# Filter transposes of an FFT-convolution kernel: quarter TensorE tiles in place of half tiles, with a new emission order

## The chip, the cores and the metric

The kernel runs on one core of a Trainium2 chip. The metric is the device time of one execution in microseconds (us). Every run of a changed kernel was made beside runs of the kernel before on the same chip. The kernel before took 230.56 to 233.16 us in its first three runs, a spread of about 1%, so a difference of 1% needs several runs; where a verdict below has an interval, it is a 95% one.

## The reference, cut to what matters

One sequence of 2048 positions and 640 channels goes through two branches, and a gate for each position mixes them.

```python
def _A_ref(q, k, v, shift_k, ssm_k, ssm_D):      # branch A
    k_shift = ...                                 # 4-tap causal convolution of k
    kv  = k_shift * v
    kf_f = rfft(pad(ssm_k))                       # filter: 640 channels x 2048 taps
    y   = irfft(rfft(pad(kv)) * kf_f)[:S]         # long convolution, length 4096
    return q * (y + kv * ssm_D)

def _B_ref(x, w1, w2, w3, w4):                    # branch B
    h  = gelu(layernorm(x) @ w1)
    x1 = x + concat(shifts of h) @ w2
    return x1 + gelu(layernorm(x1) @ w3) @ w4

g = sigmoid((x * gate_w).sum(-1))                 # x = q
return g * A + (1 - g) * B
```

The change concerns the filter `ssm_k`, which arrives with channels on the partitions and is needed with time on the partitions before its DFT.

## The kernel before

The program first registers its steps (a name, what it may run on, its dependences, its buffers) and then emits them in the order of one long string, `ORDER`. An entry such as `mx2.2/V` is "step mx2.2, on VectorE"; `P` is TensorE, `A` ScalarE, `G` GpSimd, `S` the engine that issues DMA; further numbers are buffers. Every engine runs its own entries strictly in that sequence.

The filter lies in a tile of 5 blocks of 128 channels (`a`). A position splits into block half `g`, an index of 64 and `t1`. A transpose loads its input as the stationary operand of TensorE:

```python
HN = RG.rearrange("p (k a g t) -> p k t g a", k=DT, g=2, t=T1)   # 64 columns, 32 elements (64 bytes) apart
for a in range(DT):                                              # 5 blocks
    def f_trh(e, a=a, pb=pb):
        for t1 in range(T1):                                     # 16
            for g in range(2):                                   # the two column halves of the array
                nc.tensor.transpose(out=ps16(pb)[64 * g:64 * g + 64, t1 // 8, (t1 % 8) * P:(t1 % 8 + 1) * P],
                                    in_=HN[:, a, t1, g, :], identity=IDN[:])
    tr = pl.add("trh%d" % a, {PE: 16 * 64 + (0 if a else 600)}, f_trh, [ldh[a], n_idn], [pb], mode="c")
    trhe.append(evac("trhe%d" % a, ...))                         # PSUM to SBUF, VectorE or ScalarE
```

The first DFT step uses the array in four quarters of 64 rows by 64 columns, and all five evacuations must be done before it:

```python
for g in range(2):
    for C in range(2):
        nc.tensor.matmul(ps(pb)[64 * C:64 * C + 64, g, i * n:(i + 1) * n],
                         lhsT=F1[64 * g:64 * g + 64, s, 64 * C:64 * C + 64],
                         rhs=src[64 * g:64 * g + 64, s, ds], ...)
```

## Time and profile before

| | before |
|---|---|
| time, median of 3 runs | 232.64 us (230.56 to 233.16) |
| span of the profiled execution | 230.4 us |
| TensorE busy in the span | 211.5 us |
| filter transposes | 160, in 80 pairs |
| first matmul of the first DFT step | 18.89 us |
| first key-value product of VectorE ends | 57.8 us |

The times and instructions of the profile come from one execution. "L687" is a line of the kernel. Three lines of the TensorE groups between 5 and 27 us, kernel before: line, operation, tiles, count, then busy us and the mean ns of one, then idle time ahead of the group and what ended it.

```profile
L687 PE MATMUL PS<-IDN,RG 128*64 128x128 bf16 x160 | 9.4, 289 | 2.0 <-DMA RG<-in_A_ssm_k_dram 2.0
L564 PE MATMUL PS<-XNT,R 128*128 128x512 bf16 x23 | 6.0, 380 | 0.1
L535 PE MATMUL PS<-IDN,XN 128*128 128x128 bf16 x40 | 2.9, 220 | 0.0
```

L687 is the filter transpose, L535 the transposes of the layer norm, L564 the matmuls with w1. The only idle time of these is for the filter to arrive. Two more lines of the page will be compared later: the clock granted to TensorE in 40 slices, in tenths, and the DMA queue that brings instructions (number, MB, share).

```profile
PEclk9999999999999999999999999999999999999998
...
q8 instruction: 14, 0.23, 0.4%
```

### The profile page before, as it was taken

Reading aid. Unit: us, or ns where it says so; the run is one execution under the profiler, and the core shown is the slowest. Engines: PE = TensorE matmul, PEld = TensorE weight load, DVE = VectorE, ACT = ScalarE, POOL = GpSimd, SP = SyncE. Lnnn points to the kernel's source line nnn. Section 1 sums busy time; section 2 is a strip of 40 time slices with the busy share of each in tenths; the row PEclk is TensorE's granted clock in tenths of the full one; section 3 lists DMA queues with packets and bytes.
Section 4 is the critical chain, followed back from the end, with each engine's and each line's share of the span. In section 5 each row is a group of like instructions: output and inputs, shape, how many; then the busy total and the mean of one; then the engine's idle time right before and its main releaser. Section 6 shows DMA issues by size and latency. Waiting matters only on the chain.

```text
span 230.4 us, 4825 instructions
## 1 busy us (share of the span) xinstructions
PE 211.5 (92%) x1831; PEld 119.1 (52%) x1849; DVE 187.4 (81%) x324; ACT 158.2 (69%) x238; POOL 50.6 (22%) x129
## 2 busy tenths in 40 slices
PE   6698999999989999999999998889799999999960
PEld 6694556455644476544545564233246554567640
DVE  6869988579999999999997986968849994065874
ACT  6669993859695990289979433889875886545431
POOL 2654388632640695000023000000000000000000
PEclk9999999999999999999999999999999999999998
DMA  5999989999999999999899999999979965699896
GB/s 204 396 392 172 300 160 258 233 216 308 383 188 281 299 152 292 270 209 300 256 303 379 314 318 345 257 270 351 351 281 311 370 208 179 207 405 349 275 369 242
DMA packets 51095, 65.39 MB, mean 284 GB/s; under 512 B 20608, under 2 KB 37761, under 8 KB 50688
## 3 DMA queue, kind: packets, MB, share of 16 engines
q1 hardware_dynamic: 51072, 65.09, 96.7%
q8 instruction: 14, 0.23, 0.4%
q14 instruction: 9, 0.07, 0.1%
HBM read 37.03 MB, written 18.35 MB: 240 GB/s over the span
## 4 chain that ended last, share of the span: by engine, by line
PE 50%; DMA 28%; DVE 15%; SPq 3%; issue 3%; ACT 1%; DVEq 0%
PE PS L751 14%; PE PS L764 13%; DMA CJ<-in_A_q_dram 6%; PE PS L847 6%; DMA XNT<-XN 6%; PE PS L564 6%; DMA GHD<-SX 5%; DMA RK<-in_A_k_dram 4%; PE PS L687 4%; DMA RK<-GHD 4%; DVE RK L819 3%; PE PS L712 3%; DMA RG<-in_A_ssm_k_dram 3%; PE PS L653 2%; DVE QX L660 2%
## 5 line engine op out<-in xcount | busy, mean ns | idle before, releaser
L751 PE MATMUL PS<-XNT,W 128*128 128x512 bf16 x228 | 54.8, 380 | 2.0 <-DVE RK L819 0.8
L764 PE MATMUL PS<-W,RG 128*128 128x320 bf16 x384 | 55.7, 299 | 0.5 <-DVE QX L770 0.5
L316 ACT CAST SX<-PS 128x1024 bf16<-128x1024 f32 (+1 forms) x51 | 45.6, 933 | 13.4 <-PE PS L847 11.0
L764 PEld LDWEIGHTS <-RG 128*128 128x128 bf16 x384 | 36.5, 98 | 19.9 <-issue 6.0
L751 PEld LDWEIGHTS <-W 128*128 128x128 bf16 x240 | 21.8, 97 | 31.1 <-issue 7.6
L755 ACT ACTIVATE RG<-PS 128x512 bf16<-128x512 f32 x48 | 27.9, 607 | 10.7 <-PE PS L751 10.3
L770 DVE SCALAR_TENSOR_TENSOR QX<-PS,ZG,QX 128x320 bf16<-128x320 f32 x32 | 17.1, 544 | 11.7 <-PE PS L764 11.7
L898 DVE TENSOR_TENSOR SX<-SX,R 128x2048 bf16<-128x2048 bf16 x20 | 23.8, 1219 | 3.1 <-DMA R<-R 2.8
L564 PE MATMUL PS<-XNT,R 128*128 128x512 bf16 x94 | 23.1, 379 | 0.4 <-issue 0.2
L653 PE MATMUL PS<-R 128*128 128x320 bf16 x160 | 23.4, 299 | 0.0
L320 DVE CAST SX<-PS 128x1024 bf16<-128x1024 f32 (+1 forms) x17 | 18.0, 1063 | 4.0 <-PE PS L712 3.2
L942 ACT ACTIVATE RK<-PS,ZG 128x640 bf16<-128x640 f32 x16 | 11.7, 793 | 13.1 <-PE PS L932 5.9
L823 DVE TENSOR_TENSOR RK<-RK 128x1280 bf16<-128x1280 bf16 x24 | 20.0, 833 | 0.5
L653 PEld LDWEIGHTS <-R 128*128 128x128 bf16 x160 | 15.2, 98 | 8.2 <-issue 2.0
L819 DVE TENSOR_TENSOR RK<-RK,CJ 128x1280 bf16<-128x1280 bf16 x24 | 19.1, 816 | 0.0
L316 ACT CAST KV<-PS 128x1024 bf16<-128x1024 f32 x16 | 16.0, 1019 | 2.2 <-PE PS L847 2.1
L493 ACT ACTIVATE RG<-QX 128x640 bf16<-128x640 bf16 x16 | 11.8, 739 | 8.1 <-DVE QX L660 4.0
L520 DVE TENSOR_SCALAR XN<-QX,MV,RS 128x640 bf16<-128x640 bf16 x32 | 14.9, 476 | 2.5 <-DMA XNT<-XN 2.4
L318 ACT ACTIVATE R<-PS 128x1024 bf16<-128x1024 f32 x12 | 11.8, 1026 | 6.2 <-PE PS L847 4.6
L847 PEld LDWEIGHTS <-M 64*64 64x64 bf16 x320 | 7.6, 105 | 16.2 <-issue 7.1
L847 PE MATMUL PS<-RK,M 64*64 64x512 bf16 x160 | 13.1, 386 | 2.6 <-DMA RK<-GHD 1.7
L564 PEld LDWEIGHTS <-R 128*128 128x128 bf16 x100 | 9.0, 97 | 10.6 <-issue 1.3
(107 smaller groups left out, 269.5 us busy)
## 6 DMA issues: line engine op xcount, KB each, us to landing
GHD<-SX SPq DMA_DIRECT2D x8, 640.0 KB, 6.0
GXD<-SX SPq DMA_DIRECT2D x8, 640.0 KB, 4.7
RK<-GHD SPq DMA_DIRECT2D x4, 1280.0 KB, 8.8
RK<-GXD SPq DMA_DIRECT2D x4, 1280.0 KB, 7.6
R<-R SPq DMA_DIRECT2D x8, 640.0 KB, 7.5
VD<-KV SPq DMA_DIRECT2D x4, 1280.0 KB, 5.7
RK<-VD SPq DMA_DIRECT2D x8, 640.0 KB, 6.5
W<-in_B_w_dram SPq DMA_DIRECT2D x2, 1920.0 KB, 12.4
```

What stands on the lines that cost most here:

```text
L316: nc.scalar.copy(out=o, in_=i)
L320: nc.vector.tensor_copy(out=o, in_=i)
L564: nc.tensor.matmul(ps(pb), lhsT=lhsT, rhs=XNT[:, xb.idx, k, :], start=(k == 0), stop=(k == DT - 1))
L653: nc.tensor.matmul(ps(pb)[:, j, 0:DH], lhsT=gst_ap(k, s), rhs=W2[:, k, j * DH:(j + 1) * DH], start=(k == 0), stop=(k == DT - 1))
L751: nc.tensor.matmul(ps(pb), lhsT=W3[:, k, f0 * P:(f0 + 1) * P], rhs=XNT[:, xb.idx, k, :], start=(k == 0), stop=(k == DT - 1))
L755: gns.append(pl.add("g2.%d.%d" % (c, f0), {A: act_p(512)}, lambda e, f0=f0, pb=pb, gb=gb: nc.scalar.activation(out=GTP[:, gb.idx, f0 % 4, ...
L764: nc.tensor.matmul(ps(pb)[:, 0:DH], lhsT=GTP[:, gbs[f // 4].idx, f % 4, i * P:(i + 1) * P], rhs=W4[:, f, j * DH:(j + 1) * DH], start=(f == ...
L770: nc.vector.scalar_tensor_tensor(out=x, in0=ps(pb)[:, 0:DH], scalar=OMG[:, s:s + 1], in1=x, op0=ALU.mult, op1=ALU.add)
L819: m = pl.add("km%d.%d.%d" % (c, u, j), {V: dve(2 * D, .52)}, lambda e, src=src, cj=cj, tb=tb: nc.vector.tensor_tensor(out=TMP[:, tb.idx].r ...
L823: prev = pl.add("ka%d.%d.%d" % (c, u, j), {V: dve(2 * D, .52)}, lambda e, tb=tb: nc.vector.tensor_tensor(out=acc, in0=acc, in1=TMP[:, tb.i ...
L847: nc.tensor.matmul(pt[64 * C:64 * C + 64, R, :], lhsT=M3[64 * R:64 * R + 64, m, :], rhs=rhs_fn(R, C), start=start, stop=stop)
L898: nc.vector.tensor_tensor(out=PQ[:, qb.idx], in0=XS[:, sb.idx].unsqueeze(1).to_broadcast([P, 2, 1024]), in1=HH[:, hhb.idx, u], op=ALU.mult)
```

## The change

Its intent: the transposes use the same quarter tiles as the DFT, four at a time instead of two, and stream 64 columns instead of 128, so they should take about half as long. The whole emission order was made anew with the smaller cost.

```diff
             for t1 in range(T1):
-                for g in range(2):
-                    nc.tensor.transpose(out=ps16(pb)[64 * g:64 * g + 64, t1 // 8, (t1 % 8) * P:(t1 % 8 + 1) * P],
-                                        in_=HN[:, a, t1, g, :], identity=IDN[:])
-        tr = pl.add("trh%d" % a, {PE: 16 * 64 + (0 if a else 600)}, f_trh, [ldh[a], n_idn], [pb], mode="c")
-        trhe.append(evac("trhe%d" % a, lambda a=a: HT[:, :, a * P:(a + 1) * P],
-                         lambda pb=pb: ps16(pb).rearrange("p j (t d) -> p (j t) d", t=8), 2048, [tr], [pb], rate=.52))
+                for R in range(2):
+                    rs = slice(64 * R, 64 * R + 64)
+                    for g in range(2):
+                        nc.tensor.transpose(out=ps16(pb)[64 * g:64 * g + 64, R, t1 * 64:(t1 + 1) * 64],
+                                            in_=HN[rs, a, t1, g, :], identity=IDN[rs, rs])
+        tr = pl.add("trh%d" % a, {PE: 16 * 58}, f_trh, [ldh[a], n_idn], [pb], mode="q")
+        trhe.append(evac("trhe%d" % a, lambda a=a: HT[:, :, a * P:(a + 1) * P].rearrange("p t (r d) -> p r t d", r=2),
+                         lambda pb=pb: ps16(pb).rearrange("p r (t d) -> p r t d", t=T1), 2048, [tr], [pb], rate=.52))
 ORDER = """
-idn/G bpi/V is/G cs/V iw/G cw/V ang1/V and1/V sin1.1/A ...     (910 entries)
+idn/G warm/P/0 q1/S bpi/V is/G cs/V iw/G cw/V ang0/V ...       (the same 910 steps, another sequence, 59 of them on another engine)
```

Not shown: an estimate (`iss=1000.0`) for eight reloads of scratch tensors, which only served to make the order.

## The prediction

> **What bounds the kernel now.** I read the page's busy shares first, then its DMA queues, then the chain of waits in order of time, the timeline of the first 20 us, and last a table of busy time by stretch.
>
> The page, kernel before: engines, then the DMA queues.
>
> ```profile
> PE 211.5 (92%) x1831; PEld 119.1 (52%) x1849; DVE 187.4 (81%) x324; ACT 158.2 (69%) x238; POOL 50.6 (22%) x129
> ...
> q1 hardware_dynamic: 51072, 65.09, 96.7%
> ```
>
> TensorE is busy 92% of a 230.4 us span and the DMA engines almost all of it. Neither alone says what a saved microsecond is worth, so I go by time. Chain of waits in order of time (start, length, what), up to the first DFT step:
>
> ```profile
> 1.65 5.84 DMA RG<-in_A_ssm_k_dram
> 7.49 0.04 issue
> 7.53 3.80 PE PS L687 x62
> 11.33 0.66 PE PS L535 x10
> 11.99 5.50 PE PS L687 x96
> 17.52 1.24 DVE KV L320
> 18.76 0.14 issue
> 18.89 0.74 PE PS L712 x16
> ```
>
> L687 is the filter transpose, L712 the first DFT step. From 7.5 to 18.9 us the path is: the first filter block arrives, 160 transposes run in one queue, the last evacuation follows, and only then may the DFT start (it depends on all five evacuations). So the changed instructions lie wholly on the path here. The timeline of TensorE in the same stretch and, for comparison, of a short burst of DFT step 1 with 128-column matmuls:
>
> ```profile
> 7.53 3.80 PE L687 MATMUL PS<-IDN,RG 128*64 128x128 bf16 x64 [1.99 <-DMA RG<-in_A_ssm_k_dram]
> 11.93 5.56 PE L687 MATMUL PS<-IDN,RG 128*64 128x128 bf16 x96
> 31.78 0.63 PE L712 MATMUL PS<-KV,F 64*64 64x128 bf16 x20
> ```
>
> The bracket is the idle time before the group and what ended it. The first two lines are 59 and 58 ns for one transpose. The third line, quarter tiles with the same 128 columns streamed, needs 31 ns for one, tail of the last included. Table by stretch (sum, then busy us of each engine, clock, DMA share, GB/s):
>
> ```profile
> 10.00:15.00 5.00, 5.00 (x92) 4.83 (x88) 4.49 (x6) 3.54 (x9) 2.38 (x7) 1.00 1.04 395
> 15.00:20.00 5.00, 4.21 (x73) 3.49 (x72) 2.67 (x5) 4.07 (x6) 2.77 (x15) 1.00 1.11 281
> 20.00:25.00 5.00, 5.00 (x36) 2.38 (x36) 4.90 (x18) 4.97 (x7) 2.37 (x7) 1.00 0.83 198
> 100.00:120.00 20.00, 19.62 (x167) 9.21 (x166) 19.39 (x31) 18.29 (x30) 0.58 (x3) 1.00 0.95 270
> 160.00:180.00 20.00, 18.23 (x172) 8.79 (x166) 15.52 (x15) 14.97 (x20) 0.00 (x0) 1.00 0.93 316
> ```
>
> At 10 to 15 us TensorE has no gap; VectorE and ScalarE have some at 15 to 20, both waiting for L687. After that TensorE is full up to about 140 us, and VectorE nearly so (19.39 of 20). From 140 to 180 TensorE loses some 3.6 us in 40 to waits on DMA.
>
> **What the Trainium skill says.** "TensorE: Matmul & The Clock Gate", section "LDWEIGHTS (loading the stationary operand)": a weight load takes columns divided by 1.2 ns, whatever the rows; 64 columns give an estimate of 53 ns. The same page, section "The mechanism": weight loads overlap running matmuls only when the row group differs. The trace agrees with both read together: the starts of the old transposes come in pairs (the two column tiles start within about 5 ns of each other), a pair every 108 to 112 ns. That is 53 ns of load plus 128 columns at 2.4 GHz, 53 ns, one after the other: both tiles use all 128 rows, so no load hides. In the DFT burst at 31.8 us the starts come in fours (3 to 4 ns apart), and where nothing else holds them the next four come 55 to 56 ns later: there the load is hidden. "TensorEngine Tiling (Array Packing)", section "Key Properties", says that a change of tile mode drains the array; the start of the first transpose of the other mode (L535) comes 206 ns after the last pair of L687, about 100 ns more than the spacing of pairs, so this trace agrees and the size is small. The same page's "Gotcha 1: PSUM Pressure" says that two row tiles can't use the same PSUM bank at once; the new code gives each row half its own bank, so I expect no cost.
>
> **The change part by part.**
>
> 1. Transposes. Removed: 160 instructions of 128 rows x 64 columns with 128 columns streamed. By starts they take 5 blocks x 16 pairs x 110 ns = 8.8 us (the group's busy time is 9.4 us with tails). Added: 320 instructions of 64x64 with 64 columns streamed, in 80 rounds of four. A round has 53 ns of load and 27 ns of streaming. If the load is hidden as in the DFT burst, a round takes 55 ns: 16 x 55 = 0.88 us a block, 4.4 us in all. If it isn't, 80 ns: 1.28 us a block, 6.4 us in all. I take about 0.95 us a block with its start, 4.7 us: 4.1 us less TensorE work.
>
> 2. What the path gains. The blocks are not there for the taking. By issue plus time to landing, the five filter loads of before arrive at 7.5, 8.8, 10.9, about 12.2 and 13.4 us; two of the q loads (9.6 us the next) lie between. The new queue order is h1, h0, h2, q, h4, h3, the same bytes up to the last, so 13.4 us stays. The last block then runs 13.4 to 14.35. VectorE empties it after the block before it: 14.35 + 1.22 (the VectorE copy of 128x2048) = 15.6, plus 0.15 issue gives the first DFT matmul at about 15.75 us, against 18.89. One LN transpose group (0.7 us) falls into the wait. The gain on the path is thus about 3.1 us, and not 4.1: some 1 us of the saved work becomes waiting for the filter. With a slower VectorE queue ahead of the last copy (statistics at about 1.05 us each) it is 2.4 us.
>
> 3. Mode switches. The normal-mode transpose groups of the LN still stand between the filter blocks, in the old order and in the new, so the number of switches in the start is equal: about zero.
>
> 4. Evacuation. Same 2048 elements and same engine kinds, output in runs of 64 elements in a different nesting; two of five go to ScalarE (1.86 us) instead of one, which takes 1.2 us off VectorE where it matters. No cost on the path, as they are not the last.
>
> 5. New order, and the larger issue estimate for eight reloads of the scratch tensors. The estimate is only a number that placed instructions; nothing runs longer for it. 59 of 910 steps change engine: 28 go from VectorE to ScalarE and 22 back. The tail (inverse DFT, reloads, stores) is almost the same sequence. I count this part as 0 +- 1.5 us.
>
> Sum: of 3.1 us at the first DFT step, TensorE can carry most as far as about 140 us, as it has hardly a gap there. But the DMA starts no earlier than before and has as much to move, so I let a third be lost at DMA waits: -2.0 us. I add -0.8 us because an order made with the new costs should use the freed start. 232.64 - 2.8 = 229.8 us.
>
> **Rivals.**
>
> A. Everything carries through: 3.1 to 4 us, 228.6 to 229.5 us, or lower with a better order. For it: TensorE 92% busy, full for 120 us after the start. Against: the DMA figures.
>
> B. The DMA takes it back. For it: 96.7% share, the chain spends 28% of the span in DMA, 8.7 us at 143 us in LN transposes and 8.8 us at 158 us in a reload of the filter spectrum, and the last 25 us are reloads and stores. Against: bandwidth of only 198 GB/s at 20 to 25 us beside 395 at 10 to 15, so the share is partly packets waiting for one another. This gives 231.5 to 233 us.
>
> C. The small transposes don't run four at a time: with twice the instructions at 24 ns each, which the gate's one-column matmuls need in the chain (0.48 us for 20), or a little more, they would take 7.7 to 9 us, about the same as now. Against it: starts 3 to 4 ns apart in the DFT burst. It gives 232 to 234 us, with the order deciding.
>
> D. ScalarE becomes the bound just after the start: it is full (4.97 of 5 us) at 20 to 25 us and gets two more copies. It could lose 1 us of the 3.1: 230.5 us.
>
> **Range and chances.** A and the main line together have about 65%, B and D 27%, C 5%. Three runs of before spread from 230.56 to 233.16 us, which adds about 1 us either way. I predict 229.8 us, 226.8 to 232.6 eight times in ten. Faster by over 2% means under 228.0 us, and needs the whole 3.1 us and some 1.5 us from the order: 0.24. Within 2%: 0.73. Slower by over 2% would need a bad order: 0.03.
>
> **What would show it.** Right: the transpose group has 320 matmuls in about 5 us of busy time, starts in fours some 55 ns apart; TensorE shows short waits for the filter load between blocks; the first DFT matmul starts at 15.3 to 16.5 us; TensorE's busy time is 4 to 5 us lower; the span is 2 to 4 us shorter. Wrong in step 1 if the rounds take 80 ns or more; in step 2 if the DFT starts later than 16.5 us though the filter landed by 13.5; in the sum if the DFT starts 3 us earlier and the lead is gone by 60 us (rival D) or between 140 and 170 us (rival B), seen as longer TensorE waits there, or if it grows beyond 3 us, which would be the order's doing.

## The result, and the profile after

The changed kernel took 239.07, 239.23, 239.00 and 238.19 us, a median of 239.03 us; the kernel before took 231.96 us (median of 4) on the same chip. The ratio is 1.030, with a 95% interval of 1.023 to 1.037: slower. Ratios here and below are the mean time of one kernel's fast runs over that of the other's fast runs of the same rounds, so not quite the ratio of the medians that are quoted.

The page of the kernel after: engines, clock and instruction queue.

```profile
PE 215.6 (91%) x2009; PEld 120.7 (51%) x2009; DVE 183.5 (77%) x316; ACT 163.4 (69%) x241; POOL 57.7 (24%) x134
...
PEclk9755899999999999999999999999999999999997
...
q8 instruction: 15, 0.25, 0.4%
```

TensorE's busy time rose by 4.1 us where 4 to 5 us less had been expected. The start has slices of half clock, and one more instruction fetch was made. The chain of waits in order of time (start, length, what), kernel after; L689 is now the filter transpose and L714 the first DFT step:

```profile
7.74 3.74 PE PS L689 x125
11.48 1.18 PE PS L535 x10
12.66 1.56 PE PS L689 x49
14.23 0.13 issue
14.36 3.73 PE PS L689 x97
18.09 2.47 issue
20.56 0.66 PE PS L689 x14
21.21 1.18 PE PS L535 x10
22.40 1.28 PE PS L714 x13
23.71 2.28 PE PS L564 x5
```

Three things differ from before. The transposes fill the time from 7.74 to 21.21 us (they had ended near 17.5). There is a pause of 2.47 us that the chain ascribes to no other engine and to no transfer ("issue": the engine waited for nothing that this view shows). And the ten layer-norm transposes beside them take 1.18 us where the chain of before had 0.66. The DFT starts 3.4 us later than before; by its second burst (25.92 us against 20.75) the delay is 5.2 us. The TensorE groups of 5 to 27 us, kernel after:

```profile
L689 PE MATMUL PS<-IDN,RG 64*64 64x64 bf16 x320 | 9.8, 291 | 4.8 <-issue 2.5 <-DMA RG<-in_A_ssm_k_dram 2.2
L564 PE MATMUL PS<-XNT,R 128*128 128x512 bf16 x8 | 3.1, 532 | 0.0
```

320 transposes have 9.8 us of busy time, where I had predicted about 5. By the starts of the single records they do run four at a time: four start within 8 to 12 ns of each other. But a round of four starts every 110 ns, as a pair did before: 80 rounds x 110 ns = 8.8 us, the same as the old 80 pairs x 110 ns. The spacing is the same 110 ns between 7.8 and 8.7 us as between 14.5 and 18 us, and the clock recorded for these two differs (full to 8.77 us, half from there to 25.84); the table by stretch shows it coarsely (columns: sum, busy us of TensorE, of its weight loads, of VectorE, ScalarE and GpSimd, then the clock, DMA share and GB/s). Kernel after:

```profile
5.00:10.00 5.00, 2.77 (x90) 2.54 (x87) 4.07 (x13) 2.65 (x5) 2.24 (x5) 0.88 1.01 354
10.00:15.00 5.00, 4.87 (x140) 4.48 (x136) 3.43 (x7) 3.90 (x6) 0.99 (x6) 0.50 1.03 395
15.00:20.00 5.00, 3.09 (x115) 2.96 (x108) 1.42 (x2) 1.87 (x1) 3.42 (x15) 0.50 1.06 369
```

So the round is held by something that does not follow TensorE's clock. Between 15 and 20 us VectorE (1.42 of 5 us busy) and ScalarE (1.87) starve.

### The profile page after: what moved, and what is told of

Read it like the earlier page. It is cut to its first block, busy times and chain, and to the rows that moved or that the text cites. A ratio compares the mean times of both kernels' runs of the same rounds, so it can differ in the third digit from the quotient of the medians.

```text
span 236.9 us, 5176 instructions
## 1 busy us (share of the span) xinstructions
PE 215.6 (91%) x2009; PEld 120.7 (51%) x2009; DVE 183.5 (77%) x316; ACT 163.4 (69%) x241; POOL 57.7 (24%) x134
## 4 chain that ended last, share of the span: by engine, by line
PE 50%; DVE 22%; DMA 17%; issue 5%; SPq 3%; ACT 1%; DVEq 0%
PE PS L766 13%; PE PS L753 10%; PE PS L564 7%; PE PS L849 6%; DMA RK<-in_A_k_dram 6%; DVE RK L821 5%; DVE RK L825 5%; DMA CJ<-in_A_q_dram 4%; PE PS L653 4%; PE PS L689 4%; DMA R<-R 4%; PE PS L714 3%; DMA RG<-in_A_ssm_k_dram 3%; DVE QX L660 2%; DVE RK L948 2%
## 5 line engine op out<-in xcount | busy, mean ns | idle before, releaser
L753 PE MATMUL PS<-XNT,W 128*128 128x512 bf16 x240 | 56.2, 380 | 0.9 <-ACT RG L757 0.8
L316 ACT CAST SX<-PS 128x1024 bf16<-128x1024 f32 (+1 forms) x54 | 47.5, 925 | 12.0 <-PE PS L849 7.3
L757 ACT ACTIVATE RG<-PS 128x512 bf16<-128x512 f32 x48 | 27.4, 607 | 14.8 <-PE PS L753 14.7
L772 DVE SCALAR_TENSOR_TENSOR QX<-PS,ZG,QX 128x320 bf16<-128x320 f32 x32 | 17.0, 545 | 14.1 <-PE PS L766 14.0
L564 PE MATMUL PS<-XNT,R 128*128 128x512 bf16 x100 | 24.1, 391 | 0.0
L821 DVE TENSOR_TENSOR RK<-RK,CJ 128x1280 bf16<-128x1280 bf16 x24 | 20.0, 842 | 0.0
L653 PEld LDWEIGHTS <-R 128*128 128x128 bf16 x160 | 15.4, 98 | 8.0 <-issue 1.6
L316 ACT CAST KV<-PS 128x1024 bf16<-128x1024 f32 x17 | 16.9, 1016 | 1.9 <-PE PS L849 1.9
L320 DVE CAST SX<-PS 128x1024 bf16<-128x1024 f32 (+1 forms) x14 | 14.8, 1066 | 2.9 <-PE PS L714 1.8
L564 PEld LDWEIGHTS <-R 128*128 128x128 bf16 x100 | 9.4, 99 | 12.2 <-issue 2.7
L714 PE MATMUL PS<-KV,F 64*64 64x128 bf16 (+1 forms) x256 | 13.4, 314 | 1.8 <-DVE QX L660 1.0
L689 PE MATMUL PS<-IDN,RG 64*64 64x64 bf16 x320 | 9.8, 291 | 4.8 <-issue 2.5
```

The source lines that it names most:

```text
L316: nc.scalar.copy(out=o, in_=i)
L564: nc.tensor.matmul(ps(pb), lhsT=lhsT, rhs=XNT[:, xb.idx, k, :], start=(k == 0), stop=(k == DT - 1))
L653: nc.tensor.matmul(ps(pb)[:, j, 0:DH], lhsT=gst_ap(k, s), rhs=W2[:, k, j * DH:(j + 1) * DH], start=(k == 0), stop=(k == DT - 1))
L689: nc.tensor.transpose(out=ps16(pb)[64 * g:64 * g + 64, R, t1 * 64:(t1 + 1) * 64], in_=HN[rs, a, t1, g, :], identity=IDN[rs, rs])
L753: nc.tensor.matmul(ps(pb), lhsT=W3[:, k, f0 * P:(f0 + 1) * P], rhs=XNT[:, xb.idx, k, :], start=(k == 0), stop=(k == DT - 1))
L757: gns.append(pl.add("g2.%d.%d" % (c, f0), {A: act_p(512)}, lambda e, f0=f0, pb=pb, gb=gb: nc.scalar.activation(out=GTP[:, gb.idx, f0 % 4, ...
```

## The experiments

They had to answer three questions: why a round takes 110 ns, what the pauses are, and what the two halves of the change, transposes and order, cost by themselves. Fifteen experiments ran (e11 repeats the kernel of e1). Those called wrong on purpose compute wrong values in the filter or the key convolution; their instructions and waits are of the same kind, and only their times are used. (They passed the comparison with the reference all the same, so its tolerance does not vouch for these terms.)

### e1 and e11: the new transposes alone

The kernel after with the `ORDER` string of before. e11 is the same kernel again, as e1 had two disturbed runs.

> The quarter-tile transposes in the old emission order. If the transposes and what they do at the start cost the time (a late instruction block, a lower clock, rounds no shorter than the old pairs), this run is as slow as the changed kernel, about 236 to 239 us (ratio 1.02 to 1.03), with the first DFT matmul at 22 us or later. If the new order costs it, this run is within 1% of the kernel before. Rounds of four transposes start 110 ns apart in either case.

> The quarter-tile transposes in the old order once more, for a ratio from fast runs: 234 to 236 us, 1.01 to 1.02, with VectorE some 4 us more idle before its first key-value product than in the kernel before.

e1: 235.34, 233.48 us, and two runs of the slow state (239.83 us at a mean clock of 0.95, 312.29 us at 0.679), too few for a ratio; the two fast runs lie 1.7 and 3.5 us above the 231.81 us of the kernel before beside them. e11: 235.27 to 238.07 us in four fast runs, median 236.38; ratio 1.019, interval 1.013 to 1.025. So the transposes alone make the kernel slower, by some 4.4 us in e11. TensorE's timeline of e1 (start, length, group, idle time before it):

```profile
10.91 1.25 PE L535 MATMUL PS<-IDN,XN 128*128 128x128 bf16 x10
12.09 5.50 PE L689 MATMUL PS<-IDN,RG 64*64 64x64 bf16 x177
20.04 0.66 PE L689 MATMUL PS<-IDN,RG 64*64 64x64 bf16 x15 [2.46 <-issue]
20.63 1.25 PE L535 MATMUL PS<-IDN,XN 128*128 128x128 bf16 x10
22.11 1.28 PE L714 MATMUL PS<-KV,F 64*64 64x512 bf16 x16 [0.23 <-DVE KV L320]
23.32 1.88 PE L564 MATMUL PS<-XNT,R 128*128 128x512 bf16 x5
```

The pauses stand at the same places as in the kernel after: a short one after 177 transposes (starts 0.41 us apart in place of 0.11, so 0.3 us lost) and one of 2.46 us after 305. Another order doesn't move them. The two layer-norm groups take 0.52 us more each than in the timeline of before (0.73 us). The first transpose starts at 7.08 us, 0.45 earlier than before. Pauses 2.9 us in all, slower layer-norm transposes 1.0 us, less these 0.45 us: 3.4 us, against the 3.2 us by which the DFT starts later. The next two groups, also slower than before, bring the delay to 4.4 us at 25.1 us, and of that 3 to 4 us are left at the end of the span's last inverse DFT (4.0 us in e11, 3.0 in e1).

Are the slow groups the lower clock? A row of the table by stretch of e1 and of e11 seems to speak against it. e1:

```profile
15.00:20.00 5.00, 2.58 (x95) 2.46 (x92) 0.77 (x1) 3.42 (x5) 2.79 (x15) 1.00 1.18 298
```

The same stretch of e11:

```profile
15.00:20.00 5.00, 2.59 (x95) 2.46 (x92) 0.77 (x1) 3.42 (x5) 2.55 (x14) 0.50 1.13 285
```

The view says 1.00 in one run and 0.50 in the other, and TensorE is busy for the same 2.58 and 2.59 us; the DFT starts at 22.1 us in both, and the layer-norm groups take the same time. But the difference is one of the record. The clock records in the packed trace (start, length, clock) begin only at 24.63 us in e1, and the view counts a stretch without a record as full clock. The pace tells what it was. In the kernel before, whose records begin at 10.42 us with full clock, the first matmuls of the program take twice the time of later ones of the same size:

```profile
1.52 4.02 PE L458 MATMUL PS<-IDN 128*128 128x128 bf16 x36 [1.52 <-POOL IDN L453]
```

These start 107 ns apart, and the layer-norm transposes from 11.26 us on, with 128 columns too, 56 ns. In e1 both the first matmuls and both layer-norm groups start 107 ns apart: it ran at half clock until 24.63 us, as e11 did by its records (full from 5.46 to 8.88 us, half to 25.94, then full). So the half clock is what slows the groups beside the pauses. In e1 that is 1.0 us in the layer-norm transposes and another 1.2 us in the first DFT and w1 groups; half a microsecond of it is not the change's doing, as the first layer-norm group takes 1.25 us in e9, e10, e13 and e15 too, which have the old transposes.

All traces of this case divide the same way. In the ten kernels with the old half tiles or e6's full array the clock is full from 4.4 to 13.6 us on, and stays so past 60 us; in the seven with quarter tiles, of either order, only from 23.6 to 26.8 us on. The pauses are not what brings it down: in e7 below TensorE works without a gap from 1.52 us on, and its clock falls from full to half at 9.97 us, before any pause. Why the quarter tiles don't bring it up is not settled by these runs.

### e3, e4 and e6: what holds a round at 110 ns

The stationary operand is read with a step of 64 bytes. e3 (kernel before) and e4 (kernel after) read 64 neighbouring columns instead, and e6 (kernel before) does one full-array transpose of 128 columns 32 bytes apart in place of a pair. All three are wrong on purpose.

```diff
 e3, e4:
-    in_=HN[:, a, t1, g, :]
+    in_=HNl[:, a, (2 * t1 + g) * 64:(2 * t1 + g + 1) * 64]        # e4: rows rs
 e6:
-    for g in range(2): nc.tensor.transpose(out=...[64 * g:64 * g + 64, ...], in_=HN[:, a, t1, g, :], ...)
+    nc.tensor.transpose(out=...[:, ...], in_=HNl[:, a, t1::16], ...)
```

> The kernel before with each transpose loading 64 neighbouring columns in place of 64 columns 64 bytes apart (a wrong result, on purpose). Theory of the stride: the strided load itself lasts about 110 ns for 64 columns and sets the pair's period; then pairs come about 55 ns apart, the group's busy time falls from 9.4 to about 5 to 6 us. Theory of the prediction (load 53 and stream 53 one after the other): pairs stay at about 110 ns.

> The changed kernel with neighbouring columns loaded (a wrong result, on purpose). Theory of the stride: rounds of four fall from 110 to about 55 ns, unless the clock is low. Theory that four small transposes can't run together: rounds stay at about 110 ns. The wait for an instruction block stays, or grows, as the instructions are used up faster.

> Old order, 80 transposes over the whole array, each loading 128 columns 32 bytes apart (rows come out in another order: a wrong result, on purpose). If a strided load is set by the columns loaded one after the other, one takes about 220 ns and the group about 18 us, and the kernel is slower by several us. If the load of 128 columns goes in four parts side by side, one takes about 110 ns or less and the group is no longer than before, with half the instructions.

With neighbouring columns the old pairs of e3 start every 56 ns in the last three blocks and the new rounds of e4 every 53 to 54 ns. (In its first two blocks e3 shows 107 ns; it ran at half clock there, since the layer-norm group behind them starts at 107 ns and drops to 56 ns at 10.9 us.) The 110 ns were the strided read of the stationary operand: at full clock in the old pairs, and at both clocks in the new rounds. This agrees with the Trainium skill, "Advanced Engine Details and Errata", section "SBUF Cachelines", which gives 16-byte lines and a penalty where each access falls in another line; here it is a factor of two at 64 bytes. e6 at 32 bytes needs 61 to 63 ns for all 128 columns at full clock (107 ns in a half-clock stretch); whether the shorter step or the undivided array makes it quick was not tried apart.

e3's timeline of TensorE:

```profile
6.72 3.72 PE L687 MATMUL PS<-IDN,RG 128*64 128x128 bf16 x64 [1.18 <-DMA RG<-in_A_ssm_k_dram]
10.37 0.96 PE L535 MATMUL PS<-IDN,XN 128*128 128x128 bf16 x10
11.26 2.96 PE L687 MATMUL PS<-IDN,RG 128*64 128x128 bf16 x96
...
15.63 0.75 PE L712 MATMUL PS<-KV,F 64*64 64x512 bf16 x16 [0.75 <-DVE KV L320]
```

And e4's, from its third block on:

```profile
10.87 0.90 PE L689 MATMUL PS<-IDN,RG 64*64 64x64 bf16 x49
13.84 1.92 PE L689 MATMUL PS<-IDN,RG 64*64 64x64 bf16 x128 [2.07 <-issue]
20.31 0.42 PE L689 MATMUL PS<-IDN,RG 64*64 64x64 bf16 x15 [4.55 <-issue]
...
21.85 1.35 PE L714 MATMUL PS<-KV,F 64*64 64x128 bf16 x16
```

e4 is the telling one. Its transposes have 5.4 us of busy time in all against 9.8 in the kernel after, and yet its long pause ends at 20.31 us, where that one's had ended at 20.56. The saved time went into the pauses: 2.07 and 4.55 us. Its time, with the new order in it as well, is 239.86 us (ratio 1.038, interval 1.025 to 1.050, two runs), no better than the kernel after. In e3, with half as many instructions, there are no such pauses and the DFT starts 3.3 us earlier than in the kernel before.

But e3 is not faster either: 231.28 us over 18 runs, ratio 0.9996 (0.9966 to 1.0025). In its profile the lead falls from 2.6 us at the first w1 matmul to 1.2 us at 38 us (TensorE waits 0.77 us at 31.7 us, for the load of a row that the DFT needs) and is between 1 and 2 us from there. e6, whose DFT starts at 16.06 us, took 229.17 and 231.88 us, ratio 0.990 (0.982 to 0.998): of nearly 3 us perhaps 2. So an earlier DFT was worth nothing measurable in e3 and perhaps 2 us in e6; what parts the two is not known.

### e7, e8 and e12: what the pauses are

The pauses are 128 transposes apart (after 177 and after 305; the expectations count from zero and write "before 177 and 305"). A transpose is a weight load and a matmul, so this is 256 instructions, and the Trainium skill, "Advanced Engine Details and Errata", section "ISA Cache", gives a line of 16 KB or 256 instructions. The trace agrees on both: the instruction queue moves 16384 bytes at a time, and in the kernel after one of these fetches starts at 12.0 us and one at 18.1 us, the second with the start of the long pause. The theory: TensorE has used up its instructions and waits for the next 256. The rival: the pause is bound to work at that place, such as a DMA transpose that shares the queue.

```diff
 e7 (e1 with 16 more matmuls ahead of the transposes):
-    for _ in range(36)
+    for _ in range(52)
 e8 (e1 with the DMA transpose "tri" issued later):
-    q6/S q5/S tri/S w1m/G ...        ... hw2/S/0 z0/V/5
+    q6/S q5/S w1m/G ...              ... hw2/S/0 tri/S z0/V/5
 e12 (e1 with 64 more one-column matmuls ahead):
-    nc.tensor.matmul(ps(wb)[:, 0:P], ..., rhs=IDN[:]) for _ in range(36)
+    nc.tensor.matmul(ps(wb)[:, 0:(P if j < 36 else 1)], ..., rhs=IDN[:, 0:(P if j < 36 else 1)]) for j in range(100)
```

> Quarter-tile transposes in the old order, with 16 more warm-up matmuls (32 more instructions) before them. Theory of the instruction block: the two long pauses, now before transposes 177 and 305 of 320, come 16 transposes earlier, before 161 and 289, and the last is about as long. Rival (the wait is for data, a PSUM bank or the filter's arrival): the pauses stay where they are.

> Quarter-tile transposes in the old order, with the long DMA transpose of the DFT matrix moved some 8 DMA starts later in the queue. If its traffic is what delays the fetch of the instruction block, the pause before transpose 305 falls from 2.5 us to under 1 us. If the fetch simply takes its time from the block's start, the pause stays at 2 us or more.

> Quarter-tile transposes in the old order, with 64 matmuls of one column (128 more instructions, about 1.6 us, in a stretch in which TensorE waits for the filter) after the warm-up. The block borders then come 64 transposes earlier, before transposes 113 and 241. If a block becomes usable some 6.2 us after the one before it was begun, the pause before 241 is shorter than 2.5 us (1 to 2 us) and none comes after it, and the first DFT matmul starts 0.8 to 1.5 us earlier than the 22.1 us of the run without them; ratio 1.005 to 1.015 in place of 1.02. If the pauses hang on the transposes and not on the instruction count, they stay before 177 and 305 at 0.4 and 2.5 us.

TensorE's timeline in e7, around the long pause:

```profile
11.76 5.05 PE L689 MATMUL PS<-IDN,RG 64*64 64x64 bf16 x161
19.27 1.09 PE L689 MATMUL PS<-IDN,RG 64*64 64x64 bf16 x31 [2.46 <-issue]
```

The same in e8:

```profile
11.61 5.16 PE L689 MATMUL PS<-IDN,RG 64*64 64x64 bf16 x177
19.03 0.65 PE L689 MATMUL PS<-IDN,RG 64*64 64x64 bf16 x15 [2.27 <-issue]
```

And both pauses of e12:

```profile
12.88 0.33 PE L689 MATMUL PS<-IDN,RG 64*64 64x64 bf16 x5 [2.55 <-issue]
...
19.62 2.42 PE L689 MATMUL PS<-IDN,RG 64*64 64x64 bf16 x79 [1.91 <-issue]
```

In e7, 16 more matmuls ahead move the pause from 15 transposes before the end to 31 before the end: by exactly 16. In e8 the long pause stays at the same transpose with the DMA transpose gone from there; the rival falls. (Its short pause is gone, but TensorE had waited longer for the filter first.) e12 missed its expectation. It was to put the border where the fetch would be done in time. The second border came where expected, after 241 transposes, but the first after 123 and not 113: the ten layer-norm transposes between the blocks count as instructions too, which I had forgotten. Both pauses are long (2.55 and 1.91 us) and the DFT starts at 23.45 us, 1.3 us later than in e1: an earlier border brings no time when the supply itself is the limit. Its four runs have a median of 235.21 us, ratio 1.016 (1.006 to 1.027), e7's only run 233.67 us and e8's 236.68 us.

The supply can be read from all of them as the time from the first instruction after one pause to the first after the next: 6.20 us in the kernel after (14.36 to 20.56), in e1 and in e7, 6.47 in e4, 6.74 in e12. So 256 TensorE instructions come in some 6.2 to 6.7 us here. The instruction queue's own packets agree. In each of these kernels TensorE goes on 2.3 to 2.5 us after a fetch starts, of which the packet itself takes about 1 us, and the fetches start 6.1 to 6.6 us apart, in e4 even though TensorE has been out of work for 2.07 us by then (it stops at 15.76 us, the fetch starts at 17.83). So it is the start of the fetch that is late, and not its transfer; what sets that start is not shown. The new transposes at 110 ns a round use 256 in 3.5 us and those of e4 in 1.9 us; both must wait. The old pairs use 256 in 64 x 110 ns = 7.0 us, just slower than the supply, and so the kernel before has no such pause.

### e2, e5 and e13: the new order alone, and mending its waits

e2 is the kernel before with the `ORDER` string of after. e5 moves one entry of it later on VectorE; e13 moves two more.

```diff
 e5 (e2 with):
-    xt0.3.0/S/1/0 mx2.2/V kb1/S/1 ...  xn1.2/V/2 mx2.1/V
+    xt0.3.0/S/1/0 kb1/S/1 ...          xn1.2/V/2 mx2.2/V mx2.1/V
 e13 (e5 with):
-    m3i3/G mx1.3/G xn0.9/V/0 st0.11/V rs0.10/G q6/S ...  W1.2.2/P/3/0 mx1.0/G ...  ka0/S/1 gt.2/P/1/0 z2/V/1
+    m3i3/G xn0.9/V/0 st0.11/V rs0.10/G mx1.3/G q6/S ...  W1.2.2/P/3/0 gt.2/P/1/0 mx1.0/G ...  ka0/S/1 z2/V/1
```

> The old column-tile transposes in the new emission order. If the transposes cost the time: 230 to 233 us, ratio 0.99 to 1.005, no long idle time of TensorE between transposes. If the order costs it: 236 to 239 us, with the lead lost after 25 us. If both do, 234 to 236 us.

> Old transposes and new order, with one VectorE step (the copy of the third shift group of token chunk 2) put three places later in VectorE's queue, after the steps that it held up for 3.1 us in the run with the new order alone. If the order's cost is VectorE work pushed behind that wait, about 2 to 3 us come back: 231.5 to 233 us, ratio below 1.01. If the order costs by its DMA sequence or elsewhere, it stays at 234 to 235.5 us.

> The kernel before with its own transposes and the new emission order, mended at the three places where the trace of the order-only kernels showed a wait of VectorE before the first key-value product: the maximum of block 2.2 is queued later on VectorE, TensorE's gate product of block 2.2 comes right after its W1 group and not after five others, and GpSimd's row sum of block 0.10 comes ahead of the maximum that had held it back. Theory 1, what the order costs is VectorE's early waits: VectorE's idle time before the first key-value product falls from 13.1 us in the order-only kernel to 9 to 10.5 us, and the time to 231 to 232.5 us, a ratio under 1.006 to the kernel before. Rival, the order loses later as well, where TensorE and VectorE both are nearly full: the idle time before the first product falls and the time stays at 234 to 235.5 us. Second rival: the waits only move on to the next product in the queue, as in the kernel with the maximum moved alone, and neither falls.

e2: 234.85 us, ratio 1.016 (1.008 to 1.024). So the order costs about as much as the transposes; the two add to 3.5%, and both together were measured at 3.0%. The two longest waits of VectorE between 26 and 47 us, from its timeline in e2:

```profile
31.65 1.26 DVE L520 TENSOR_SCALAR XN<-QX,MV,RS 128x640 bf16<-128x640 bf16 x2 [2.53 <-POOL RS L513]
...
43.30 0.29 DVE L599 COPY R<-R 32x512 bf16<-32x512 bf16 x1 [3.13 <-ACT R L571]
```

In e5:

```profile
33.12 1.27 DVE L520 TENSOR_SCALAR XN<-QX,MV,RS 128x640 bf16<-128x640 bf16 x2 [2.51 <-POOL RS L513]
...
45.70 0.16 DVE L587 COPY ZG<-PS 128x4 f32<-128x4 f32 x1 [3.87 <-PE PS L578]
```

In e13:

```profile
31.69 1.47 DVE L520 TENSOR_SCALAR XN<-QX,MV,RS 128x640 bf16<-128x640 bf16 x2 [1.08 <-POOL RS L513]
...
45.73 0.69 DVE L320 CAST SX<-PS 128x512 bf16<-128x512 f32 x1 [3.56 <-PE PS L712]
```

In e2, L599 (mx2.2) stands in VectorE's queue before ScalarE can have its input, and all that follows waits. With it moved (e5) the next entry waits just as long for TensorE's gate product L578, which the order places behind five w1 groups; with that moved too (e13) the next one waits for a DFT part of TensorE, placed behind the same groups. e5: 235.43 us, ratio 1.012 (1.007 to 1.017). e13: 235.13 us, ratio 1.015 (1.008 to 1.021). VectorE's idle time before its first key-value product is 10.7 us in the kernel before, 13.1 in e2, 14.9 in e5 and 14.1 in e13 (of which e5 and e13 have over 1 us because their filter came later in the profiled run). Theory 1 of e13 fails, and its second rival holds: the wait only moves on, since it is TensorE's sequence that keeps VectorE from having work.

### e14 and e15: which half of the order loses

The two orders spliced at the first key-value product (57 to 61 us), with the old transposes.

```diff
 e14: entries of before's ORDER up to kv0/V/0, then what is left in the sequence of the new ORDER
 e15: entries of the new ORDER up to kv0/V/0, then what is left in the sequence of before's ORDER
```

> The kernel before with its own transposes; the emission order is that of before up to the first key-value product, and from there on the remaining steps in the new order. Theory 1, the new order loses before the first key-value product: the product ends near 58 us as before and the time is 231 to 232.5 us, a ratio under 1.006. Rival, it loses later: the product ends near 58 us and the time is 233.5 to 235.5 us. A seam that fits badly would also be slower, with a new wait just after 58 us.

> The other half: the kernel before with its own transposes, the new order up to the first key-value product, and from there on the remaining steps in the order of before. Theory 1: the product ends near 60 us and the time is 234 to 235.5 us, a ratio of 1.012 to 1.02. Rival, the new order loses later: the product ends near 60 us and the time is 231 to 232.5 us all the same.

e14: median 233.66 us, ratio 1.010 (1.006 to 1.013, 14 runs). e15: 235.07, 235.90, 237.97 us and a slow run of 238.69; ratio of the fast ones 1.014 (1.009 to 1.018). The product ends at 56.7 us in e14, as early as before for a filter 0.9 us earlier, and at 61.5 us in e15. Each half is slower than the kernel before. Theory 1 alone (all before the product) and the rival alone (all after it) both fall. The ratios add to 2.4%, more than e2's 1.6%, so the splice itself may cost something, as e14 names. Two waits in e15's TensorE timeline, before and at the splice:

```profile
50.12 0.65 PE L579 MATMUL PS<-GWT,XNT 128*128 128x1 bf16 x20 [1.92 <-DMA XNT<-XN]
59.78 2.52 PE L654 MATMUL PS<-R 128*128 128x320 bf16 x11 [2.04 <-ACT R L572]
```

The first is the new order's own, as e2 has it too (1.50 us at 48.03 us); the second may be the splice's, as e2 waits only 0.30 us ahead of that group. What remains is that the new order loses 1.6% as a whole (e2), and that neither half is free of loss; how much belongs to each is open.

### e9 and e10: is VectorE the bound in the middle?

After 60 us VectorE is busy for nearly the whole of each slice until its last key-value product. If it were the bound, less work for it should shorten the span. e9 leaves out eight of its additions (wrong on purpose); e10 moves six multiplications to GpSimd (right result).

```diff
 e9:
-    lambda e, tb=tb: nc.vector.tensor_tensor(...)                       # ka: add one tap
+    lambda e, tb=tb, j=j: None if j == 2 else nc.vector.tensor_tensor(...)
 e10 (with six km*.0 entries as /G and the adds reordered to fit):
-    nc.vector.tensor_tensor(...)                                        # km: multiply by one tap
+    (nc.gpsimd if e == G else nc.vector).tensor_tensor(...)
```

> The kernel before without 8 of the 24 additions of the key shift on VectorE (a wrong result, on purpose): 8 x 0.83 = 6.6 us less VectorE work, 5 to 6 us of it before the last key-value product. If VectorE is what the stage from 57 to 117 us waits for, the last product ends 4 to 6 us earlier and the kernel is 3 to 6 us faster, ratio 0.975 to 0.987. If TensorE (full there too) sets the pace, under 1 us comes of it.

> The kernel before with 6 of those multiplications (one in each half chunk from the second chunk on) on GpSimd, which is idle there: a right result. If VectorE is the bound and GpSimd does one in under 5 us without slowing VectorE, 4 to 5 us of VectorE work go and the kernel is 2 to 4 us faster. If the two engines get in each other's way, VectorE's instructions get longer while GpSimd runs and nothing is won, or it is slower.

e9 takes 6.6 us from VectorE and gives 0.6 us, which is not clear of zero: 231.4 us over 20 runs, ratio 0.9975 (0.9948 to 1.0003). So VectorE's work alone is not the bound; in e9 TensorE is busy 19.2 to 19.95 us of each 20 between 60 and 120 us, and what lead there is goes at 138 us in a wait of 2.09 us for a transfer. This explains how a delay can pass through while a lead does not: two engines and the transfers are each nearly full, and all must come earlier for the end to. It is an argument from these traces, not shown by a run that frees all at once. e10 takes 246.21 us, ratio 1.060 (1.054 to 1.066). Its page:

```profile
L813 DVE TENSOR_TENSOR RK<-RK 128x1280 bf16<-128x1280 bf16 x24 | 19.8, 826 | 9.3 <-POOL RK L809 8.5
...
L809 POOL TENSOR_TENSOR RK<-RK,CJ 128x1280 bf16<-128x1280 bf16 x6 | 18.8, 3128 | 17.3 <-DVE RK L813 13.6
```

A multiplication takes 3128 ns on GpSimd, about 820 on VectorE, and VectorE waits 8.5 us for one of them. Of eight further multiplications that VectorE kept (L804, mean 1524 ns in place of 819) the three that overlap one of GpSimd's took 1.9 to 3.1 us, and the other five about 0.82 us.

## Why the prediction was wrong

I predicted 229.8 us (2.8 us less); the change made it 7.1 us more (239.03 against 231.96), outside the range, and "slower" had 3%.

- **Step 1, the transposes.** It failed, and the failed reading is the sentence "That is 53 ns of load plus 128 columns at 2.4 GHz, 53 ns, one after the other". The 110 ns of a pair were a strided read of the stationary operand (e3: 56 ns without the stride at full clock), so a quarter-tile round, which reads with the same stride, is no shorter. The term "0.88 us a block, 4.4 us in all" measured 16 x 110 ns = 1.76 us a block, 8.8 us in all, and the 4.1 us less of work were zero. Rival C had the size (7.7 to 9 us) for another reason: it said that the four would not run together, and they do. The trace that the prediction read held a warning: its layer-norm transposes (L535) also use all 128 rows, load 128 columns and stream 128, and start every 56 ns, so a load can hide there. (The starts within a pair are also not "within about 5 ns" throughout: they lie 0 to 42 ns apart.)
- **The missing terms.** The sum has no entry for instructions. Twice the number of them in the same time asks 256 per 3.5 us of a supply that gives 256 in some 6.2 us. That made the pauses, 2.9 us in e1. It has none for the clock either, which stays at half until 23.6 to 26.8 us with the quarter tiles and costs e1 some 2.2 us. Together they make up the delay of 4.4 us at 25.1 us in e1; e11's ratio is a loss of about 4.4 us. No run takes the two apart in the final time. In e4, where the transposes do take about half the time, which is what step 1 wanted, the pauses took all of it: even with step 1 right the change would not have gained.
- **Step 2, the gain on the path.** The DFT started at 22.33 us and not at 15.75. (The last filter load landed at 14.14 us, 0.7 us later than assumed; that is the smaller part.) Its own limit was well read, though: in e3, where the transposes are fast and no pause occurs, it starts at 15.63 us.
- **Step 3, mode switches.** Held as far as the traces go: from the last round before the first layer-norm group to the first round after it 1.42 us pass in e1 and 1.43 us in e9, which has the old transposes, both at half clock.
- **Step 4, the evacuation.** Held: the last one costs TensorE 0.23 us of waiting in e1 against 0.74 in the kernel before, and no wait for it is seen in the kernel after.
- **Step 5, the order, "0 +- 1.5 us".** It failed on size: 1.6% of 232 us is 3.6 us (e2). "The tail ... is almost the same sequence" was true, but the first 60 us and the middle were not, and both halves lose (e14, e15). An in-order VectorE queue that is filled for a start that doesn't come, and TensorE groups placed ahead of what VectorE needs, show as waits of 2.5 and 3.1 us.
- **The sum, "a third be lost at DMA waits".** Too hopeful: e3 really has the 3.1 us at the DFT and keeps none of it beyond the noise (ratio 0.9996). Rival B (the DMA takes it back, 231.5 to 233 us) comes nearest to e3's 231.28 us; that it is the DMA that takes the lead is not shown.

Three things stay open: why the clock stays at half for so long with the quarter tiles, how the order's loss divides, and which of the full engines and transfers takes e3's lead in its second half. No version tried here beats the kernel before by a clear margin with a right result.

## What to carry to other kernels

Before you cut instructions into smaller ones, count them against the supply: this TensorE received 256 instructions in some 6.2 us, and small ones that run faster than that end in pauses marked "issue" at fixed counts; adding a few instructions ahead and seeing the pause move by that number is a cheap proof. Check a clock of 1.00 at the start of a view against the pace of a matmul that you know, since a missing record counts as full. When two explanations give the same duration (load plus stream, or strided load), change the stride before you build on either. And test a new emission order apart from the change that it was made for, since delays pass through a kernel whose engines are all nearly full and leads do not.

## What the Trainium skill lacked or had wrong

- "TensorE: Matmul & The Clock Gate", section "LDWEIGHTS (loading the stationary operand)": the time of a load depends on the columns alone there. The stride is missing: loads with a step of 64 bytes kept pairs and rounds at 110 ns, neighbouring columns at 53 to 56 ns (e3, e4); 128 columns with a step of 32 bytes took 61 to 63 ns at full clock (e6).
- The same page, section "The mechanism": it says that a load overlaps a running matmul only when the row group differs. In e3 column-half pairs over all 128 rows started every 56 ns at full clock, with 128 columns to stream (an estimate of 53 ns from that page's clock), and so did the layer-norm transposes of the kernel before, so their loads were hidden without another row group. (The section also names a background weight buffer, which the prediction left out.)
- "Advanced Engine Details and Errata", section "ISA Cache": the size of a line fits, but the page gives no pace of refilling. Here 256 TensorE instructions came in 6.2 to 6.7 us, and the next 256 were not there in time.
- The same page, section "SBUF Cachelines": it speaks of a penalty without a size; here it was a factor of two for a step of 64 bytes in a stationary operand.
